# An attention and two-MoE kernel: merged float64 conversion, paired reciprocals, router dots over eight steps, an earlier gather

## The chip, the cores and the metric

The kernel runs on one core of a Trainium2 chip. A core has five engines with instruction queues of their own, which here are called PE (TensorE, the matrix unit), DVE (VectorE), ACT (ScalarE), POOL (GpSimd) and SP (SyncE, which here only issues DMA transfers). An engine works its queue in order and waits on semaphores for the others. The metric is the device time of one execution in microseconds, lower is better.

## The reference

```python
scores = scale * np.matmul(q, k.transpose(0, 1, 3, 2))      # q, k, v: 4 x 8 heads x 576 x 64
scores = np.where(mask, scores + bias[None], -1000000000.0) # causal window of 128, ALiBi slopes
attn = np.exp(scores - np.max(scores, axis=-1, keepdims=True))
attn = attn / (np.sum(attn, axis=-1, keepdims=True) + 1e-09)
x = np.matmul(attn, v)                                      # -> 2304 tokens x 512
a = x @ w_a; b = x @ w_b                                    # 512 -> 1536, weights in float64
x = (a * b @ w_out).astype(np.float32)                      # 1536 -> 512
logits = x @ w_gate + modality_bias[modality_id]            # 8 experts
e_idx = np.argmax(logits, axis=1)                           # one expert per token
gate_w = softmax(logits)[np.arange(N), e_idx]
out[mask] = gate_w[mask, None] * (np.maximum(x[mask] @ w1[e], 0.0) @ w2[e])   # for each expert e
```

## The kernel before

The 2304 tokens are 18 tiles of 128, taken in 7 chunks of 3, 2, 2, 3, 3, 3 and 2 tiles. Attention of a chunk is cut into items (a pair of heads and a tile). An item passes through: score_mm (PE), score_sel and score_max (DVE: mask and row maximum), score_exp (ACT: exponential p and its row sum), score_inv (DVE: 1e-9 added to the sum, then the reciprocal, both on the tile mx), the transpose ps_p (PE), its copy pc (ACT, DVE), a masked select pt (POOL), the product ps_o with v (PE), its scaled copy u (DVE and ACT), and for chunk 0 a transpose ps_ot back into xr, the input of the first MoE.

Each chunk then takes 12 steps j, one for each 128 columns of d_ff. A step has 24 matmuls mm_ab (a and b against xr, into ps_ab), asb (ACT copies a), gf (DVE multiplies it with b), g (ACT and DVE split gf in two parts), and mm_out of the step before into the accumulators. The attention of the next chunk runs between these matmuls. Chunk 0's attention has nothing to run beside, and is called the front. After it, slot0 runs chunk 0's steps.

The weights come as float64. On the chip they are read as pairs of 32-bit words and made into float32 bit by bit on DVE: `one` shifts and masks the high word (L429), `two` and `three` merge the sign and the low word into it (L433, L437). ACT then copies the result rounded (L444) and DVE subtracts that from it (L445), so that a weight is the sum of two parts. f64_ops does it for a tile of 128x512; wab_jobs makes a list of these jobs for a and b of a step, the two loads of which (wraw) SP issues one after the other (L450). In the front conv_step takes jobs off the list, in chunk 0 slot0 takes those of the step j+2 (NCV is 2). The bit tiles f64f stand in the tag "x2" with three buffers.

The router's logits of a chunk are computed during the steps of the next chunk. rd_fetch loads two experts' gate weights, sent to all partitions (wgt, 512 KB, on SP's queue, in the tag "wo" with four buffers, which it shares with the w_out tiles). rd_dot multiplies and sums them with every token tile on DVE (L596), rd_fin picks the expert. That takes the steps j = 0 to 3. Chunk 3 also writes zero rows through SP (x2_init).

At the end the second MoE runs in units of up to 384 tokens that share an expert: gen0 prepares the first, big(u) the next. A unit loads an index list (SP), gathers its tokens with an indirect DMA (POOL), and transposes them (ps_t) for the matmuls ps_h and ps_y.

The order within the engines' queues is written out by hand in the front, and found by a tile scheduler everywhere else, which places instructions by an estimate of when they are ready. So a small edit can move instructions far from it.

## Time and the profile before

| | |
|---|---|
| three runs | 837.05, 837.06, 839.56 us; median 837.06 |
| the profiled execution's own time | 840.08 us |
| its span, first to last instruction | 838.4 us (1.7 us lie around it) |
| mean granted PE clock | 0.994 |
| busy in the span | PE 812.3 us (97%), DVE 557.2 (66%), ACT 429.8 (51%), POOL 182.1 (22%) |

Busy is the time in which an engine has an instruction under way; a PE that is busy need not be at its peak, since matmuls are pipelined and their ends are modelled. Where an engine other than PE idles it costs nothing by itself. The profiled execution is one run, longer than the median of the three.

### The profile page before, as it was taken

The page shows a single profiled execution, that of the slowest core. Times are in us where ns is not written, and L with a number is a line of the kernel's source. Part 1 is how long each engine was busy: PE and PEld are TensorE (multiplying, and loading weights), DVE is VectorE, ACT ScalarE, POOL GpSimd, SP SyncE. Part 2 cuts the span into 40 slices and gives each one's busy share as a digit, 9 for nine tenths or more (in the row PEclk, how much of TensorE's full clock was granted, in tenths as well). Part 3 has the DMA queues.
Part 4 walks back from the last instruction along what each step waited for, and adds up shares of the span by engine and source line. Part 5 has one row for each costly group of instructions (what it writes and reads, how often), then busy time and mean ns, then how long its engine had stood idle before and what let it go on. Part 6 is the DMA issues. An engine that isn't in the chain of part 4 may idle for free.

```text
span 838.4 us, 14297 instructions
## 1 busy us (share of the span) xinstructions
PE 812.3 (97%) x4770; PEld 730.6 (87%) x4770; DVE 557.2 (66%) x1699; ACT 429.8 (51%) x1144; POOL 182.1 (22%) x245
## 2 busy tenths in 40 slices
PE   8899999999999989999999999999999999999994
PEld 6788877989989979999999999999988998979893
DVE  7799996987976875568865693377376444447320
ACT  6754465647666735665556632232336444537420
POOL 5322012113222222212222111100133030115101
PEclk9999999999999999999999999999999999999998
DMA  9995445786674774444642253647328553538301
GB/s 260 339 401 188 137 140 169 206 284 200 190 213 149 186 211 131 117 120 139 180 130 89 76 186 105 200 163 223 134 82 303 193 185 123 185 117 294 123 27 40
DMA packets 67874, 145.37 MB, mean 173 GB/s; under 512 B 12047, under 2 KB 32175, under 8 KB 67792
## 3 DMA queue, kind: packets, MB, share of 16 engines
q1 hardware_dynamic: 64240, 134.64, 51.6%
q0 software_dynamic: 3552, 9.73, 3.2%
q8 instruction: 40, 0.66, 0.3%
q14 instruction: 42, 0.34, 0.1%
HBM read 122.35 MB, written 22.12 MB: 172 GB/s over the span
## 4 chain that ended last, share of the span: by engine, by line
PE 75%; issue 8%; DMA 5%; DVE 5%; ACT 3%; POOL 2%; SPq 1%; POOLq 0%; ACTq 0%; DVEq 0%
PE ps_ab L512 32%; PE acc L529 13%; PE ps_h L1129 8%; PE ps_y L1112 7%; PE ps_o L369 4%; PE acc L525 4%; PE ps_s L247 2%; DMA wgt<-in_wgt 2%; PE ps_p L297 1%; PE ps_o L334 1%; PE ps_t L934 1%; PE ps_s L243 1%; DVE junk L596 1%; ACT p L271 1%; POOL out L1119 1%
## 5 line engine op out<-in xcount | busy, mean ns | idle before, releaser
L512 PE MATMUL ps_ab<-xr,wab 128*128 128x384 f32 (+1 forms) x2016 | 345.1, 318 | 4.7 <-DVE gf L1071 3.2
L512 PEld LDWEIGHTS ps_ab<-xr,wab 128*128 128x128 f32 x2016 | 308.5, 188 | 16.9 <-DVE gf L1071 4.7
L529 PE MATMUL acc<-wo,g 128*128 128x512 f32 x540 | 143.9, 398 | 0.0
L311 POOL TENSOR_SCALAR_AFFINE_SELECT pt<-pc 128x512 fp32r<-128x512 f32 (+1 forms) x72 | 50.4, 700 | 330.1 <-DVE pc L309 189.6
L529 PEld LDWEIGHTS acc<-wo,g 128*128 128x128 f32 x540 | 96.5, 188 | 15.3
L1129 PE MATMUL ps_h<-xT,w1s 128*128 128x384 f32 x576 | 104.2, 337 | 0.0
L1112 PE MATMUL ps_y<-w2s,h 128*128 128x512 f32 x432 | 104.1, 394 | 0.0
L1129 PEld LDWEIGHTS ps_h<-xT,w1s 128*128 128x128 f32 x576 | 99.7, 188 | 1.4 <-issue 0.5
L596 DVE CUSTOM_DVE_ANT_0 junk<-x,wgt 128x512 f32<-128x512 f32 x128 | 91.8, 717 | 12.2 <-DMA wgt<-in_wgt 8.0
L1112 PEld LDWEIGHTS ps_y<-w2s,h 128*128 128x128 f32 x432 | 79.8, 188 | 15.8
L271 ACT ACTIVATE p<-p,mx 128x128 f32<-128x128 f32 x144 | 56.8, 396 | 31.3 <-DVE mx L261 30.7
L1074 ACT CAST g<-gf 128x256 fp32r<-128x256 f32 (+1 forms) x72 | 33.0, 458 | 58.2 <-DVE gf L1071 57.9
L1071 DVE TENSOR_TENSOR gf<-ps_ab,asb 128x256 f32<-128x256 f32 (+1 forms) x72 | 35.1, 487 | 38.1 <-PE ps_ab L512 34.3
L1067 ACT COPY asb<-ps_ab 128x256 f32<-128x256 f32 (+1 forms) x72 | 30.6, 424 | 58.2 <-PE ps_ab L512 57.4
L885 DVE TENSOR_TENSOR w2s<-wr,w2s 128x1024 fp32r<-128x1024 f32 x24 | 29.4, 1225 | 38.4 <-ACT w2s L884 38.1
L313 POOL TENSOR_SCALAR_AFFINE_SELECT pt<-pc 128x512 fp32r<-128x512 f32 (+1 forms) x72 | 54.7, 760 | 0.0
L885 DVE TENSOR_TENSOR w1s<-wr,w1s 128x1024 fp32r<-128x1024 f32 x28 | 34.3, 1224 | 23.9 <-ACT w1s L884 23.9
L284 ACT ACTIVATE p<-p,mx 128x128 f32<-128x128 f32 x104 | 36.0, 394 | 25.3 <-DVE mx L276 23.8
L369 PE MATMUL ps_o<-pt,vv 128*128 128x256 f32 x312 | 48.8, 290 | 0.0
...
L255 DVE COPY_PREDICATED ps_s<-upper,ps_s 128x256 f32<-128x256 uint8 x72 | 30.5, 424 | 23.8 <-PE ps_s L247 16.5
L1132 ACT ACTIVATE h<-ps_h 128x384 fp32r<-128x384 f32 x48 | 23.4, 489 | 43.7 <-PE ps_h L1129 43.7
...
## 6 DMA issues: line engine op xcount, KB each, us to landing
wo<-wo_d SPq DMA_DIRECT2D x60, 512.0 KB, 3.8
wr<-in_moe_w SPq DMA_DIRECT2D x56, 512.0 KB, 4.3
wgt<-in_wgt SPq DMA_DIRECT2D x24, 512.0 KB, 4.3
wraw<-in_moe_w_a SPq DMA_DIRECT2D x12, 512.0 KB, 8.4
wraw<-in_moe_w_b SPq DMA_DIRECT2D x12, 512.0 KB, 9.1
wor<-in_moe_w_out SPq DMA_DIRECT2D x12, 512.0 KB, 4.4
...
wo_d<-wo SPq DMA_DIRECT2D x12, 512.0 KB, 3.3
```

What stands on the lines that cost most here:

```text
L271: nc.scalar.activation(out=it.p[:, h, :], in_=it.p[:, h, :], func=AF.Exp, bias=it.mx[:, 2 + h:3 + h], scale=-1.0, accum_out=it.mx[:, 4 + h ...
L284: nc.scalar.activation(out=it.p[:, h, :], in_=it.p[:, h, :], func=AF.Copy, scale=it.mx[:, 6 + h:7 + h])
L311: nc.gpsimd.affine_select(out=it.pt[:, :, 0], in_=pc, pattern=pat + [[-1, P]], base=0, channel_multiplier=1, compare_op=ALU.is_gt, fill=0.0)
L313: nc.gpsimd.affine_select(out=it.pt[:, :, 1], in_=pc, pattern=pat + [[1, P]], base=0, channel_multiplier=-1, compare_op=ALU.is_ge, fill=0.0)
L369: nc.tensor.matmul(it.po, lhsT=a.vv[:, t + b, r].rearrange("p h d -> p (h d)"), rhs=it.pt[:, :, b, s, :], start=(i == 0), stop=(i == 5))
L512: nc.tensor.matmul(ps[:, :n], lhsT=w[:, m, r, kk * P:(kk + 1) * P], rhs=xr[:, s, kk, :n], start=(idx == 0), stop=(idx == len(terms) - 1))
L529: nc.tensor.matmul(acc[c, t], lhsT=g[:, r, t * P:(t + 1) * P], rhs=w[:, s, :], start=(j == 0 and idx == 0), stop=(j == NJ - 1 and idx == 2))
L596: nc.vector.tensor_tensor_reduce(out=junk, in0=x2[:, 0:DM], in1=wgt[:, k], scale=1.0, scalar=0.0, op0=ALU.mult, op1=ALU.add, accum_out=lgr ...
L885: nc.vector.tensor_tensor(out=dst[:, 1], in0=srcw, in1=dst[:, 0], op=ALU.subtract)
L1071: nc.vector.tensor_tensor(out=gf[:, :n], in0=psb[:, :n], in1=asb[:, :n], op=ALU.mult)
L1112: nc.tensor.matmul(pss[t], lhsT=h[:, r, f, t * P:(t + 1) * P], rhs=W2[f // 2][:, s_, f % 2, :], start=(f == 0 and i == 0), stop=(f == 7 an ...
L1129: nc.tensor.matmul(ps, lhsT=W1[f // 2][:, r, kk, (f % 2) * P:(f % 2 + 1) * P], rhs=xT[:, s_, kk, :], start=(kk == 0 and i == 0), stop=(kk ...
```

## The change

Five edits. (1) wab_jobs converts a and b of a step together: one bit tile f64f of 128x1024 (tag "ff", one buffer), four jobs instead of eight, ACT's rounded copy in one instruction. conv_step takes one job each time and leaves four. (2) In the chunks 0 and 1 (V32) two items share a tile mx, and score_inv works once for both, at the second. (3) rd_dot does one expert a step over the steps j = 0 to 7; a fetched wgt is held for two steps; rd_fin comes at j = 7. (4) big(u) issues the index load and the gather of the unit behind it at a place S_P = 10 inside its own work, and not at that unit's start. (5) The memory for the descriptors of indirect DMAs is 8192 bytes, half of before, which makes room in SBUF for the larger f64f.

```diff
     def score_sel(it):
-        it.mx = at.tile([P, 8], F32, tag="mx", bufs=4, name="mx")
+        if a.c in V32 and cur_mx:
+            it.mxp, it.half = cur_mx.pop(), 1
+        else:
+            it.mxp, it.half = at.tile([P, 2, 8], F32, tag="mx", bufs=3, name="mx"), 0
+            if a.c in V32:
+                cur_mx.append(it.mxp)
+        it.mx = it.mxp[:, it.half]
...
     def score_inv(it):
+        if it.a.c in V32:
+            if it.half:
+                m = it.mxp
+                nc.vector.tensor_scalar(out=m[:, :, 4:6], in0=m[:, :, 4:6], scalar1=1e-9, scalar2=None, op0=ALU.add)
+                nc.vector.reciprocal(out=m[:, :, 6:8], in_=m[:, :, 4:6])
+            return
...
     def wab_jobs(j):
-        fs = []
-        def sp(m):
-            if m == 0:
-                wab[j] = wab_p.tile([P, 2, 2, KD * P], F32R, tag=f"wab{j}", name=f"wab{j}")
-            f64_split(fs[m], wab[j][:, m], nc.vector)
-        r = wraw[j]
-        return (f64_ops(r[:, 0].rearrange("p k f t -> p (k f) t"), 0, fs) +
-                f64_ops(r[:, 1].rearrange("p k f t -> p (k f) t"), 1, fs) + [("s", lambda: sp(0)), ("s", lambda: sp(1))])
+        r = wraw[j].rearrange("p m k f t -> p (m k f) t")
+        st = []
+        def one():
+            f = m1.tile([P, 2, KD * P], U32, tag="ff", bufs=1, name="f64f")
+            st.append(f)
+            nc.vector.tensor_scalar(out=f.rearrange("p m n -> p (m n)"), in0=r[:, :, 1], scalar1=3,
+                                    scalar2=0x3FFFFFFF, op0=ALU.logical_shift_left, op1=ALU.bitwise_and)
+        def more(k, sc, op):
+            f = st[0].rearrange("p m n -> p (m n)")
+            nc.vector.scalar_tensor_tensor(out=f, in0=r[:, :, k], scalar=sc, in1=f, op0=op, op1=ALU.bitwise_or)
+        def sp():
+            f = st[0].bitcast(F32)
+            w = wab[j] = wab_p.tile([P, 2, 2, KD * P], F32R, tag=f"wab{j}", name=f"wab{j}")
+            nc.scalar.copy(out=w[:, :, 0], in_=f)
+            nc.vector.tensor_tensor(out=w[:, :, 1], in0=f, in1=w[:, :, 0], op=ALU.subtract)
+        return [("d", one), ("d", lambda: more(1, 0xC0000000, ALU.bitwise_and)),
+                ("d", lambda: more(0, 29, ALU.logical_shift_right)), ("s", sp)]
...
     def rd_dot(wgt, e):
-        for k in range(2):
-            for i, t, x2, lgr in rd:
+        for i, t, x2, lgr in rd:
...
         def conv_step(g):
-            if g >= CVS and len(conv) > 8:
+            if g >= CVS and len(conv) > 4:
+                conv.pop(0)[1]()
...
-            if rd and R0 <= j < R0 + E // 2:
-                wgt = rd_fetch(2 * (j - R0))
+            if rd and R0 <= j < R0 + E and (j - R0) % 2 == 0:
+                wgt = rd_fetch(j - R0)
...
+    def pre_gather(u):
+        pool = side()
+        pre[u] = (pool,) + u_gather(ld(uv, NBIG + u, E * RG - UT), 3, pool)
...
+            if ahead and n_ == S_P:
+                pre_gather(u + 1)
...
-    nc = bacc.Bacc("TRN2", target_bir_lowering=False, num_devices=1)
+    nc = bacc.Bacc("TRN2", target_bir_lowering=False, num_devices=1, dynamic_dma_scratch_size=8192)
```

Where the order moves, it is shown at three places, row by row as the instructions stand in a queue. "waits" names the semaphores (DMAHW are queue places of transfers that SP issued).

DVE in the front, where the first conversion begins; mx is the tile of an item's maxima and sums, wraw_168 are the loads of step 0, u is the scaled copy of the first product with v. Before:

```order
L261 ISA p,mx<-ps_s,m_first 128x128
L261 ISA mx 128x1
L275 TENSOR_SCALAR mx<-mx 128x2 [waits Activation_49]
L276 RECIPROCAL mx<-mx 128x2 [waits DVE_49]
L429 TENSOR_SCALAR f64f<-wraw_168 128x512 [waits DMAHW1_49]
L341 TENSOR_SCALAR u<-ps_o,mx 128x64 [waits PE_49]
```

After:

```order
L269 ISA p,mx<-ps_s,m_first 128x128
L269 ISA mx 128x1
L287 TENSOR_SCALAR mx<-mx 128x2x2 [waits Activation_49]
L288 RECIPROCAL mx<-mx 128x2x2 [waits DVE_49]
L472 TENSOR_SCALAR f64f<-wraw_168 128x1024 [waits DMAHW2_49,DMAHW1_49]
L356 TENSOR_SCALAR u<-ps_o,mx 128x64 [waits DVE_49,PE_49]
```

The add and the reciprocal stand only at the second item of a pair and do both. The conversion is twice as wide and waits for two loads instead of one; u stands behind it as before.

DVE at the start of chunk 0; wraw_197 and wraw_208 are the loads of the steps 1 and 2, ps_s is the score of an item of chunk 1, and the ISA rows with p are its maxima. Before:

```order
L429 TENSOR_SCALAR f64f<-wraw_197 128x512 [waits DMAHW5_49]
L429 TENSOR_SCALAR f64f<-wraw_197 128x512 [waits DMAHW6_49]
L429 TENSOR_SCALAR f64f<-wraw_208 128x512 [waits DMAHW7_49]
L255 COPY_PREDICATED ps_s<-upper,ps_s 128x2x128 [waits DVE_49,PE_49]
L433 SCALAR_TENSOR_TENSOR f64f<-wraw_197,f64f 128x512 [waits DVE_49] x2
L433 SCALAR_TENSOR_TENSOR f64f<-wraw_208,f64f 128x512 [waits DVE_49]
L261 ISA p,mx<-ps_s,m_strad 128x128 [waits DVE_49]
L261 ISA mx 128x1
```

After:

```order
L472 TENSOR_SCALAR f64f<-wraw_197 128x1024 [waits DMAHW6_49,DMAHW5_49]
L263 COPY_PREDICATED ps_s<-upper,ps_s 128x2x128 [waits DVE_49,PE_49]
L477 SCALAR_TENSOR_TENSOR f64f<-wraw_197,f64f 128x1024 [waits DVE_49]
L269 ISA p,mx<-ps_s,m_strad 128x128 [waits DVE_49]
L269 ISA mx 128x1
L269 ISA p,mx<-ps_s,m_strad 128x128
L269 ISA mx 128x1
L477 SCALAR_TENSOR_TENSOR f64f<-wraw_197,f64f 128x1024 [waits DVE_49]
```

Ahead of the first maximum there were six conversion instructions of 512 columns, and now two of 1024.

SP in chunk 5, at the router's fetches; wo are the w_out tiles. Before:

```order
L588 DMA wgt<-in_wgt 128x1024 [waits PE_49]
L178 DMA vr_3_5934<-in_v 128x3x128 [waits DMAHW5_49,DMAHW2_49,DVE_49]
L492 DMA wo<-wo_d 128x1024 [waits DMAHW6_49,PE_49]
L588 DMA wgt<-in_wgt 128x1024 [waits DMAHW7_49,DMAHW1_49,PE_49]
L492 DMA wo<-wo_d 128x1024 [waits DMAHW4_49,DMAHW0_49,DVE_49]
L588 DMA wgt<-in_wgt 128x1024 [waits DMAHW3_49,PE_49]
L492 DMA wo<-wo_d 128x1024 [waits DMAHW7_49,DVE_49]
L588 DMA wgt<-in_wgt 128x1024 [waits DMAHW6_49,PE_49]
```

After:

```order
L611 DMA wgt<-in_wgt 128x1024 [waits DMAHW4_49,PE_49]
L178 DMA vr_3_5832<-in_v 128x3x128 [waits DMAHW5_49,DMAHW0_49,DVE_49]
L515 DMA wo<-wo_d 128x1024 [waits DMAHW7_49,DMAHW6_49,PE_49]
L515 DMA wo<-wo_d 128x1024 [waits DMAHW1_49,PE_49]
L611 DMA wgt<-in_wgt 128x1024 [waits DMAHW4_49,DVE_49]
L515 DMA wo<-wo_d 128x1024 [waits DMAHW3_49,PE_49]
L515 DMA wo<-wo_d 128x1024 [waits DMAHW6_49,DMAHW2_49,PE_49]
L611 DMA wgt<-in_wgt 128x1024 [waits DMAHW0_49,DVE_49]
```

The fetches of wgt waited for PE before; two of the three now wait for DVE. On DVE stands at the third of them, with x the token tiles and lgr their logits:

```order
L618 ISA junk,lgr<-x_6066,wgt 128x512 [waits DVE_49]
L618 ISA lgr 128x1
L324 TENSOR_TENSOR pc<-ps_p,pc 128x2x128 [waits Activation_49]
L618 ISA junk,lgr<-x_6060,wgt 128x512 [waits DMAHW3_49,DVE_49]
L618 ISA lgr 128x1
L1090 TENSOR_TENSOR gf<-ps_ab_6363,asb 128x384 [waits PE_49]
L618 ISA junk,lgr<-x_6063,wgt 128x512 [waits DVE_49]
```

The dot that waits for a DMA is the first on the new wgt, and gf of the next step is queued behind it.

## Rows read from the trace of the kernel before

**Rows 1.** Windows: stretch, length, busy (instructions) by engine, PE clock, DMA share, GB/s.

```profile
0.00:40.00 40.00, 34.95 (x188) 26.23 (x188) 32.28 (x156) 28.15 (x100) 19.59 (x60) 0.96 0.96 295
40.00:50.00 10.00, 8.95 (x51) 7.65 (x50) 7.83 (x23) 3.85 (x14) 2.24 (x4) 1.00 1.01 408
50.00:150.00 100.00, 100.00 (x522) 81.58 (x522) 92.92 (x239) 55.56 (x158) 17.31 (x24) 1.00 0.58 189
...
150.00:350.00 200.00, 194.42 (x1320) 180.74 (x1318) 156.14 (x547) 125.75 (x390) 48.59 (x62) 1.00 0.66 192
...
sum 838.00, PE 812.30 PEld 730.63 DVE 557.25 ACT 429.77 POOL 182.10; mean PE 101.54 PEld 91.33 DVE 69.66 ACT 53.72 POOL 22.76
```

**Rows 2.** Waits of PE over the span: us in total, times, longest.

```profile
PE ps_ab L512 <- DVE gf L1071: 3.2, 3, 2.0
PE ps_t L934 <- DMA xg<-x2d,idx: 1.6, 1, 1.6
PE ps_p L297 <- ACT p L271: 1.3, 6, 0.4
...
PE ps_o L334 <- POOL pt L311: 0.7, 2, 0.5
```

**Rows 3.** Groups of DVE by shape: busy us, mean ns, idle before.

```profile
L596 DVE CUSTOM_DVE_ANT_0 junk<-x,wgt 128x512 f32<-128x512 f32 x128 | 91.8, 717 | 12.2 <-DMA wgt<-in_wgt 8.0 <-ACT x L610 2.5
L885 DVE TENSOR_TENSOR w1s<-wr,w1s 128x1024 fp32r<-128x1024 f32 x28 | 34.3, 1224 | 23.9 <-ACT w1s L884 23.9
...
L433 DVE SCALAR_TENSOR_TENSOR f64f<-wraw,f64f 128x512 uint32<-128x512 uint32 x24 | 16.1, 690 | 0.0
L445 DVE TENSOR_TENSOR wab<-f64f,wab 128x512 fp32r<-128x512 f32 x24 | 15.9, 691 | 0.6 <-ACT wab L444 0.6
L275 DVE TENSOR_SCALAR mx<-mx 128x2 f32<-128x2 f32 x72 | 15.7, 219 | 7.6 <-ACT p L271 7.5
...
L276 DVE RECIPROCAL mx<-mx 128x2 f32<-128x2 f32 x72 | 11.4, 159 | 0.9
L429 DVE TENSOR_SCALAR f64f<-wraw 128x512 uint32<-128x512 uint32 x24 | 10.6, 469 | 0.6 <-DMA wraw<-in_moe_w_a 0.6
```

**Rows 4.** Timeline of SP, 11 to 13 us: start, us, instruction.

```profile
11.38 0.38 SPq L706 DMA_DIRECT2D wg<-in_moe_w_gate  x1
12.69 0.34 SPq L707 DMA_DIRECT2D mb<-in_moe_modality_bias  x1
```

**Rows 5.** Timeline of DVE at the first conversion; in brackets idle before.

```profile
11.38 0.52 DVE L429 TENSOR_SCALAR f64f<-wraw 128x512 uint32<-128x512 uint32 x1 [0.63 <-DMA wraw<-in_moe_w_a]
```

**Rows 6.** Timeline of POOL, 17 to 19 us.

```profile
17.37 0.84 POOL L311 TENSOR_SCALAR_AFFINE_SELECT pt<-pc 128x256 f32<-128x256 f32 x1 [3.77 <-ACT pc L303]
18.17 0.41 POOL L313 TENSOR_SCALAR_AFFINE_SELECT pt<-pc 128x256 f32<-128x256 f32 x1
```

**Rows 7.** Windows: the stretch of the front with the lower clock.

```profile
18.64:22.05 3.41, 3.41 (x14) 2.94 (x13) 1.89 (x9) 1.62 (x8) 2.67 (x8) 0.50 0.99 380
```

**Rows 8.** Timeline of DVE at the start of chunk 0.

```profile
43.25 1.28 DVE L429 TENSOR_SCALAR f64f<-wraw 128x512 uint32<-128x512 uint32 x3
...
46.58 0.28 DVE L261 CUSTOM_DVE_ANT_0 p<-ps_s,m_strad 128x128 f32<-128x128 f32 x1
```

**Rows 9.** Timelines of SP, DVE and PE in chunk 3, 293 to 305 us.

```profile
293.55 0.54 SPq L588 DMA_DIRECT2D wgt<-in_wgt  x1
...
301.70 0.69 DVE L596 CUSTOM_DVE_ANT_0 junk<-x,wgt 128x512 f32<-128x512 f32 x1 [5.96 <-DMA wgt<-in_wgt]
...
302.92 2.00 PE L512 MATMUL ps_ab<-xr,wab 128*128 128x384 f32 x10 [1.97 <-DVE gf L1071]
```

**Rows 10.** DMA issues of the page: KB each, median us from issue to landing.

```profile
wgt<-in_wgt SPq DMA_DIRECT2D x24, 512.0 KB, 4.3
```

**Rows 11.** Timeline of DVE in chunk 6: two steps' gf.

```profile
593.16 0.42 DVE L1071 TENSOR_TENSOR gf<-ps_ab,asb 128x256 f32<-128x256 f32 x1 [0.87 <-issue]
...
597.38 0.42 DVE L1071 TENSOR_TENSOR gf<-ps_ab,asb 128x256 f32<-128x256 f32 x1 [2.90 <-PE ps_ab L512]
```

More of the change, by code (lines that the diff above doesn't have):

```diff
@@ L232, in attn_moe_moe2 @@
         pass
+    cur_mx = []
     def score_mm(a, t):
@@ L426, in one @@
         def one():
-            f = m1.tile([P, 4 * P], U32, name="f64f", **(dict(tag="wo", bufs=WOB) if key == "o" else dict(tag="x2", bufs=X2B)))
+            f = m1.tile([P, 4 * P], U32, tag="wo", bufs=WOB, name="f64f")
             st.append(f)
@@ L441, in f64_ops @@
         return [("d", one), ("d", two), ("d", three)]
-    def f64_split(f, w, lo_eng):
-        nc.scalar.copy(out=w[:, 0], in_=f)
-        lo_eng.tensor_tensor(out=w[:, 1], in0=f, in1=w[:, 0], op=ALU.subtract)
     def wab_load(j):
@@ L592, in rd_dot @@
     def rd_dot(wgt, e):
-        for k in range(2):
-            for i, t, x2, lgr in rd:
-                junk = m1.tile([P, DM], F32, tag="x2T", bufs=1, name="junk")
-                nc.vector.tensor_tensor_reduce(out=junk, in0=x2[:, 0:DM], in1=wgt[:, k], scale=1.0, scalar=0.0,
-                                               op0=ALU.mult, op1=ALU.add, accum_out=lgr[:, e + k:e + k + 1])
+        for i, t, x2, lgr in rd:
+            junk = m1.tile([P, DM], F32, tag="x2T", bufs=1, name="junk")
+            nc.vector.tensor_tensor_reduce(out=junk, in0=x2[:, 0:DM], in1=wgt[:, e % 2], scale=1.0, scalar=0.0,
+                                           op0=ALU.mult, op1=ALU.add, accum_out=lgr[:, e:e + 1])
     def rd_fin():
@@ L794, in conv_step @@
         def conv_step(g):
-            if g >= CVS and len(conv) > 8:
-                kd = conv[0][0]
-                for _ in range(2 if kd == "s" else 1):
-                    if conv and conv[0][0] == kd:
-                        conv.pop(0)[1]()
+            if g >= CVS and len(conv) > 4:
+                conv.pop(0)[1]()
         ns = n0 + 2
@@ L987, in V @@
                     a_pv(live.pop(g))
-        dq(jw[:4], "d")
+        dq(jw[:2], "d")
         psa = mm_ab(c, j, 0, None if j else 1)
@@ L998, in slot0 @@
                 score_exp(sg)
-        dq(jw[4:], "d")
+        dq(jw[2:], "d")
         if act:
@@ L1086, in attn_moe_moe2 @@
             a_preps(g + 1)
-            if rd and R0 <= j < R0 + E // 2:
-                rd_dot(wgt, 2 * (j - R0))
-                if j == R0 + E // 2 - 1:
+            if rd and R0 <= j < R0 + E:
+                rd_dot(wgt, j - R0)
+                if j == R0 + E - 1:
                     rd_fin()
@@ L1284, in u_small, with big @@
             in_=y[0:HT], in_offset=None, bounds_check=N - 1, oob_is_err=False))
-    S_A, S_B, S_C = 20, 27, 4
-    def big(u, after=None, cont=None):
+    S_A, S_B, S_C, S_P = 20, 27, 4, 10
+    pre = {}
+    def pre_gather(u):
+        pool = side()
+        pre[u] = (pool,) + u_gather(ld(uv, NBIG + u, E * RG - UT), 3, pool)
+    def big(u, after=None, cont=None, ahead=False):
         ev = ld(uv, u, E - 1)
-        pool = side()
-        idx, xg = u_gather(ld(uv, NBIG + u, E * RG - UT), 3, pool)
+        if u not in pre:
+            pre_gather(u)
+        pool, idx, xg = pre.pop(u)
         W1, W2 = u_w1(ev, wrq), u_w2(ev, wrq)
@@ L1313, in attn_moe_moe2 @@
     for u in range(NFIX):
-        gs = big(u, 0 if u == SAT - 1 else None, gs)
+        gs = big(u, 0 if u == SAT - 1 else None, gs, u + 1 < NFIX)
     def ldx(col):
```

## The prediction

> **What bounds the kernel now.** I read the busy time of the engines in stretches first [rows 1]. TensorE (PE) is busy for 812.30 of 838.00 us; between 50 and 150 us it is never idle. A gain can therefore come only from the places where it is idle: 5.05 us in 0-40, 1.05 us in 40-50, 5.58 us in 150-350. Second the waits of PE [rows 2], which say who ends that idle time: VectorE's product gf (3.2 us in three waits), ScalarE's p, and once the gather xg of the first unit. VectorE is busy for 557.25 us of the span, but for 32.28 of the first 40 us and for 92.92 of the 100 us of 50-150: only there, and where its work comes in bursts, can it hold PE back. Third the rows of VectorE by shape [rows 3], which price what is removed. Last the places where PE waited: the front [rows 4 to 7], the start of chunk 0 [rows 8] and chunk 3 [rows 9].
>
> **Conversion of two tiles at once.** Of 24 x 4 instructions of 512 columns, 12 x 4 of 1024 remain. The trace has no merged conversion, so its price is bounded: twice the row of 512 from above (no gain), and from below by how VectorE's subtraction grows from 512 to 1024 columns, 691 to 1224 ns [rows 3]: a fixed part of .16 us goes with each merged pair. By that the bit operations cost about .78 us (from .469) and 1.22 us (from .690), and a tile saves 4 x .16 = .63 us (0 to .63). I take .63, because the row of 1224 ns is the same kind of instruction. One tile is converted in the front, eleven in chunk 0. The Trainium skill's "VectorE: DVE Perf Modes", section "The TRN2 errata — SBUF-src ops pay a fixed extra latency per instruction", says that instructions on SBUF data pay a fixed cost apiece, measured there at about 150 cycles; the subtraction's .16 us agrees in size, so a sum by the page would be the same.
>
> What the merge costs is a wait. Before, the first bit operation needs only a's half: it starts at 11.38 us when that lands, after .63 us of idling [rows 5]. After, it waits for b's half too. SyncE's next two loads reuse the same two queue places and are issued at 11.38 and 12.69 [rows 4], so b's half lands 1.31 us after a's. Behind the waiting instruction stands u of the first pv item, which PE's transposes and ScalarE wait for; with the longer operation u comes about 1.31 + .31 = 1.6 us later.
>
> **Reciprocals in pairs.** 20 items of chunks 0 and 1 had an add (219 ns) and a reciprocal (159 ns) each [rows 3]; ten pairs go, 10 x .378 = 3.8 us of VectorE, six of them (2.3 us) in the front.
>
> **Sum for the front (0-40).** VectorE loses 1.6 us at 11.4 us and gains .63 + 2.3 = 2.9 us until 40. The loss comes first, the gain later, and PE's own items follow u. I take -0.5 us. Best case: all 2.9 us come out of PE's 5.05 us idle, -2.9. Worst: the 1.6 us stay. There is a second cost with bounds: PE's granted clock is .50, the lower of its two levels, from 18.64 to 22.05 [rows 7], after short stalls; those 3.41 us hold 1.7 us of full-speed work, so the front gets 1.7 us dearer if a later u brings one more such stretch. Ends -2.9 and +3.3.
>
> **Port.** POOL's two selects of a masked tile read SBUF. The same select takes .84 us at 17.37, while a two-input VectorE operation is under way, and .41 us at 18.17 [rows 6]. With merged operations of 1.22 us instead of .69 a select can be held .53 us longer, four times in the front: 0 to +2.1 us. I take 0, because PE waited for POOL's tiles only .7 us in two waits [rows 2]. The Trainium skill's "SBUF — State Buffer", section "Who interferes with whom", says why: the pair of ports that VectorE and GpSimd share is held for a whole instruction and the loser is blocked. By that rule alone the front would come out 2.1 us later; it is weighed below as part of a rival.
>
> **Start of chunk 0.** Before, three bit operations (1.28 us together), a select and three bit operations of the second kind stand ahead of the first max: 43.25 to 46.58 is 3.33 us [rows 8], and p behind that max makes PE wait [rows 2]. After, one bit operation of .78, the select and one of 1.22 stand there: about 2.3 us. So max comes 1.0 us earlier, and I take PE's whole 1.05 us of 40-50 [rows 1]: -1.0 (-1.05 to 0). **Rest of chunk 0:** VectorE saves 11 x .63 us and four pairs, but PE is never idle there [rows 1], so 0. The cover could go: the shared f64f has one buffer instead of three, and tile 3 is ready only just before its step. Ends -2 (waits hidden in PE's modelled busy time) and +1.
>
> **Router dots over eight steps.** A dot is .717 us [rows 3] and a short read; four or six stand in one step before, two or three after, over twice as many steps. The number is the same, so VectorE's work is too, but half the burst. PE's stalls in 150-350 lie in these bursts. Chunk 3's is the largest: the third weight fetch is issued at 293.55, behind a k load that waits for a buffer, and lands 8.15 us later; VectorE idles 5.96 us, and PE 1.97 us on gf [rows 9]. After, the second fetch still stands behind that load, but the load is free earlier, since kk comes sooner in the step, and the dots behind the fetch are half as many. I take the 1.97 us, -2.0 (-2.8 with a wait that follows from it; to 0). For the rest of the idle time in 150-350, 5.58 - 2.8 = 2.8 us, about half: -1.3 (-2.8 to 0).
>
> **What the spreading adds.** The order shows a new wait: ten of the 24 fetches now stand behind VectorE's own dots. They reuse the buffer of the fetch before them, which is held for two steps, so the fetch is issued only when its last dot is done, and the next dot is 2 to 16 instructions behind. A fetch takes 4.3 us [rows 10], plus some .4 us of issuing. So VectorE will idle for wgt in about eight places, 1 to 4 us each, 12 to 20 us in all (before, the row of the dots has 8.0 us [rows 3]). Queued behind the waiting dot are the next gf, g and max. In three-tile chunks PE's order leaves some 4 us and more before it needs that gf, and the idle time fits. In chunk 6 a step is only 4.22 us [rows 11]. There the last dot is done some 1.25 us after gf starts (.42 and .8), the fetch lands at 1.25 + 4.7 = 5.95, dot and next gf are done at 7.2, and PE needs that gf a step and two thirds after the first, at 7.0. So +0.2 there and as much in the other place of chunk 6: +0.5 in all. Lower end 0, upper end +8, if they land in 8.15 us as in chunk 3.
>
> **Units' gather.** SyncE's and POOL's order in the units is the same before and after: the index load still stands behind the weights in front of it. Only the first unit's gather moves, ahead of three scatters. The change does nothing here: 0 (ends -1.6, the whole wait for xg [rows 2], and +1.6, as much again if the halved descriptor memory slows a gather).
>
> **Sum.** -0.5 - 1.0 + 0 - 2.0 - 1.3 + 0.5 + 0 = -4.3 us against the profiled execution's own 840.08 us, so 835.8. That execution is 3.02 us above the median of the runs, 837.06. What it has more may be chunk 3's late landing itself, which costs 2.8 us: then the -2.0 is not to be had in the median run, and 837.06 - 2.3 = 834.8; else 837.06 - 4.3 = 832.8. I choose **833.5 us**.
>
> **Rivals.** (A) No change: PE is the bound, its idle time moves with the order, 834.5 to 839.6. For it: 97% busy, and gains of VectorE in chunk 0 that buy nothing. With the terms of chunks 1 to 5 at 0 and +0.5 for the new waits, 837.06 - 1.0 = 836. (B) Slower, by the new waits for weights: if the fetches land as late as at 301.70, VectorE's dots block gf past PE's need. 3.85 us more at each of the two places in chunk 6, and 1.5 to 2 in chunks 1 and 5, is +8: 833.5 + 8 = 841.5. It decides from a landing of about 5 us on; against it speaks the median of 4.3. (C) Slower in the front: u 1.6 us late, one more stretch at the lower clock, the selects held 2.1 us: +3.3 + 2.1 instead of -0.5, 839.4. The first ab matmul would come 3 us later or more. For it: the chain p, pt, u has no slack in the front; against it: VectorE makes 2.9 us good by its end. (D) More gain: 150-350 loses all its 5.6 us of idle time and the front 2.9, 837.06 - 5.6 - 2.9 + .5 = 829. For it: VectorE has less to do wherever it is late; against it: some of that idle time is ScalarE's.
>
> **How the numbers follow.** Within 0.3% (2.5 us) of 837.06 a measurement can't tell a change. My forecast (831 to 834.5) .43, D .12, A .28, B .12, C .05. So faster (under 834.5) .55, within 0.3% .29, slower .16: half of C falls within. The range takes in A whole and the front of B: 829.0 to 840.0.
>
> **What would show it.** Right: first bit operation of 1024 columns at 12.7 us and about .78 us long, the others 1.2 us; max of the first score in chunk 0 about 1 us earlier after it; PE idle under .3 us in 40-50; VectorE's idle for wgt rising from 8.0 to 12-20 us in eight or more waits, PE's wait for gf below 1.5 us. Wrong: PE waiting more than 3 us for gf with wgt landing over 5 us (B); the first ab matmul over 1 us later than before (C); merged operations of 1.38 us, twice the old, so that nothing is saved.

## The result: slower by 0.9%, and the profile after

The changed kernel took 846.74 us (median of 6 runs, 843.45 to 847.86) against 837.3 us (6 runs, 834.63 to 839.77) of the kernel before on the same chip: ratio 1.0091, 95% interval 1.0063 to 1.0118. (A ratio here is the estimate on record over all runs; the quotient of the two medians is 1.0113.) Its profiled execution took 845.16 us with a span of 843.5, 5.1 us more than the profiled execution before. The medians differ by 9.4 us, so the rows below hold little more than half of the loss; where the rest lies no kept trace shows.

The windows of the changed kernel show where PE lost it (columns as in [rows 1]):

```profile
0.00:40.00 40.00, 35.23 (x187) 26.67 (x187) 30.46 (x140) 27.70 (x98) 20.71 (x60) 0.96 0.96 291
40.00:50.00 10.00, 10.00 (x57) 8.80 (x58) 7.50 (x23) 5.24 (x21) 2.80 (x6) 1.00 1.02 409
50.00:150.00 100.00, 99.50 (x521) 81.23 (x520) 92.40 (x187) 52.82 (x142) 18.16 (x24) 1.00 0.57 193
150.00:250.00 100.00, 94.52 (x686) 86.93 (x685) 82.65 (x281) 62.66 (x195) 25.27 (x29) 1.00 0.68 205
250.00:350.00 100.00, 97.23 (x615) 90.54 (x614) 67.85 (x255) 62.68 (x196) 23.05 (x31) 1.00 0.65 176
350.00:580.00 230.00, 227.43 (x1347) 211.60 (x1346) 145.76 (x490) 107.54 (x307) 42.86 (x53) 1.00 0.44 134
```

PE's idle time is a window's length less its first number. The same windows of the kernel before give 97.25, 97.17 and 230.00 busy us for the last three. So the idle time went from 5.05 to 4.77, 1.05 to 0, 0 to .50, 2.75 to 5.48, 2.83 to 2.77, and 0 to 2.57: a gain of 1.3 us up to 50 us, as forecast, and losses of 2.7 us in 150 to 250, which holds most of chunk 1 and the first half of chunk 2, and of 2.6 us in 350 to 580, where chunk 4 starts. Chunk 3 gave nothing.

The waits of PE and the one of VectorE that matters, in the changed kernel ([rows 2] and the first row of [rows 3] before):

```profile
PE ps_ab L535 <- DVE gf L1090: 5.6, 8, 1.7
PE ps_o L384 <- POOL pt L326: 2.8, 2, 2.3
PE ps_t L953 <- DMA xg<-x2d,idx: 1.3, 2, 1.0
...
DVE junk L618 <- DMA wgt<-in_wgt: 33.5, 14, 6.9
```

VectorE waits for router weights four times as long as before, 14 times instead of 3, and PE waits for gf 5.6 us instead of 3.2. There are three places to look at. Steps 6 and 7 of chunk 1, the timelines of SP (two rows), DVE (five rows) and PE (last row), with the idle time and its releaser in brackets:

```profile
171.96 0.38 SPq L178 DMA_DIRECT2D vr<-in_v  x1
172.43 0.46 SPq L611 DMA_DIRECT2D wgt<-in_wgt  x1
...
177.97 0.69 DVE L618 CUSTOM_DVE_ANT_0 junk<-x,wgt 128x512 f32<-128x512 f32 x1 [1.68 <-DMA wgt<-in_wgt]
...
184.80 1.21 DVE L192 TENSOR_TENSOR kk<-kr,kk 128x1024 fp32r<-128x1024 f32 x1
...
187.11 0.70 DVE L618 CUSTOM_DVE_ANT_0 junk<-x,wgt 128x512 f32<-128x512 f32 x1
187.84 0.62 DVE L215 SCALAR_TENSOR_TENSOR qq<-qr,qscale,qq 64x384 fp32r<-64x384 f32 x1
...
188.64 0.42 DVE L1090 TENSOR_TENSOR gf<-ps_ab,asb 128x256 f32<-128x256 f32 x1
...
189.12 1.10 PE L535 MATMUL ps_ab<-xr,wab 128*128 128x256 f32 x7 [1.70 <-DVE gf L1090]
```

The fetch leaves at 172.43, right behind a v load (vr) that had held SP's queue for 3.7 us while it waited for VectorE, and lands 5.5 us later. VectorE loses 1.68 us at 177.97 and has no gap from there to gf: the late dots run into kk and qq, the preparation of the next keys and queries, and gf comes when PE has been idle for 1.7 us. The stall stands 11 us behind the wait that caused it.

Chunk 3, timelines of DVE, SP, DVE and PE, which answer to [rows 9]:

```profile
294.10 1.13 DVE L618 CUSTOM_DVE_ANT_0 junk<-x,wgt 128x512 f32<-128x512 f32 x1
...
295.27 0.34 SPq L611 DMA_DIRECT2D wgt<-in_wgt  x1
...
303.79 0.69 DVE L618 CUSTOM_DVE_ANT_0 junk<-x,wgt 128x512 f32<-128x512 f32 x1 [6.94 <-DMA wgt<-in_wgt]
...
305.01 1.31 PE L535 MATMUL ps_ab<-xr,wab 128*128 128x384 f32 x6 [1.07 <-DVE gf L1090]
```

The fetch is issued at 295.27, when the last dot on the weights before it is done (294.10 + 1.13): the new wait has taken the place of the k load's. And the landing is 8.5 us after the issue, as it was 8.1 us before, where the median is 4.0: the DMA engines are busy throughout (the DMA share is 1.11 in the window 290 to 295 us and 1.07 in 295 to 300), with six writes of zero rows (x2_init) and two k loads issued from 286 us on. No run took those writes away, so that they are the reason is not shown.

The start of chunk 4, timelines of DVE, POOL and PE:

```profile
382.87 1.23 DVE L192 TENSOR_TENSOR kk<-kr,kk 128x1024 fp32r<-128x1024 f32 x1
384.13 1.26 DVE L215 SCALAR_TENSOR_TENSOR qq<-qr,qscale,qq 64x384 fp32r<-64x384 f32 x2
385.42 0.42 DVE L324 TENSOR_TENSOR pc<-ps_p,pc 128x256 fp32r<-128x256 f32 x1
...
385.92 1.03 POOL L326 TENSOR_SCALAR_AFFINE_SELECT pt<-pc 128x512 fp32r<-128x512 f32 x1 [12.46 <-DVE pc L324]
...
387.00 0.63 PE L384 MATMUL ps_o<-pt,vv 128*128 128x256 f32 x3 [2.35 <-POOL pt L326]
```

Here no weight is late. kk and qq stand ahead of pc in VectorE's order, 2.5 us of work, and PE waits 2.35 us for the select behind pc. In the kernel before kk stands at 376.35, well ahead. This stall is the scheduler's order; runs 9 and 10 below, which can have no late weight, have it too.

### The profile page after: what moved, and what is told of

It is laid out like the page before. It is cut to its first block, busy times and chain, and to the rows that moved or that the text cites. A ratio compares the mean times of both kernels' runs of the same rounds, so it can differ in the third digit from the quotient of the medians.

```text
span 843.5 us, 14190 instructions
## 1 busy us (share of the span) xinstructions
PE 813.3 (96%) x4770; PEld 730.4 (87%) x4770; DVE 551.3 (65%) x1631; ACT 427.4 (51%) x1132; POOL 184.5 (22%) x245
## 4 chain that ended last, share of the span: by engine, by line
PE 69%; DVE 9%; issue 9%; DMA 7%; ACT 4%; POOL 2%; SPq 1%; POOLq 0%; DVEq 0%; ACTq 0%
PE ps_ab L535 29%; PE acc L552 11%; PE ps_y L1131 7%; PE ps_h L1148 7%; PE acc L548 4%; PE ps_o L384 4%; PE ps_s L249 2%; DMA wgt<-in_wgt 2%; DVE junk L618 2%; DMA wr<-in_moe_w 2%; PE ps_p L312 1%; PE ps_o L349 1%; DMA idx<-tab 1%; PE ps_s L245 1%; DVE qq L215 1%
## 5 line engine op out<-in xcount | busy, mean ns | idle before, releaser
L326 POOL TENSOR_SCALAR_AFFINE_SELECT pt<-pc 128x512 fp32r<-128x512 f32 (+1 forms) x72 | 52.7, 732 | 341.9 <-DVE pc L324 225.9
L618 DVE CUSTOM_DVE_ANT_0 junk<-x,wgt 128x512 f32<-128x512 f32 x128 | 91.0, 711 | 41.1 <-DMA wgt<-in_wgt 33.5
L328 POOL TENSOR_SCALAR_AFFINE_SELECT pt<-pc 128x512 fp32r<-128x512 f32 (+1 forms) x72 | 56.2, 780 | 0.0
L384 PEld LDWEIGHTS ps_o<-pt,vv 128*128 128x128 f32 x312 | 42.5, 189 | 6.1 <-POOL pt L326 3.6
L1094 DVE TENSOR_TENSOR g<-gf,g 128x256 fp32r<-128x256 f32 (+1 forms) x72 | 39.1, 542 | 12.0 <-ACT g L1093 11.7
```

The source lines that it names most:

```text
L326: nc.gpsimd.affine_select(out=it.pt[:, :, 0], in_=pc, pattern=pat + [[-1, P]], base=0, channel_multiplier=1, compare_op=ALU.is_gt, fill=0.0)
L328: nc.gpsimd.affine_select(out=it.pt[:, :, 1], in_=pc, pattern=pat + [[1, P]], base=0, channel_multiplier=-1, compare_op=ALU.is_ge, fill=0.0)
L384: nc.tensor.matmul(it.po, lhsT=a.vv[:, t + b, r].rearrange("p h d -> p (h d)"), rhs=it.pt[:, :, b, s, :], start=(i == 0), stop=(i == 5))
L618: nc.vector.tensor_tensor_reduce(out=junk, in0=x2[:, 0:DM], in1=wgt[:, e % 2], scale=1.0, scalar=0.0, op0=ALU.mult, op1=ALU.add, accum_out ...
L1094: nc.vector.tensor_tensor(out=gt[:, 1, :n], in0=gf[:, :n], in1=gt[:, 0, :n], op=ALU.subtract)
```

## The experiments

All runs stand against runs of the kernel before on the same chip (medians 838 to 840 us). "From before" means the kernel before with one edit. The table has the time (median), the ratio to before with its interval, VectorE's idle time for wgt and PE's for gf (us, in how many waits), and how many stretches of PE at the lower granted clock (.50) lie between 150 and 800 us; the last three columns are read from each run's profiled execution. The kernel before has 8.0 in 3, 3.2 in 3 and none, the changed kernel 33.5 in 14, 5.6 in 8 and none.

| run | us | ratio | idle for wgt | PE for gf | clock |
|---|---|---|---|---|---|
| 1 after, dots over 4 steps | 838.75 | 0.9995 [0.9977, 1.0012] | 9.9 in 4 | 5.4 in 4 | 1 |
| 2 before, dots over 8 | 849.58 | 1.0120 [1.0091, 1.0148] | 34.3 in 15 | 4.0 in 3 | 3 |
| 3 before, merged conversion | 840.54 | 1.0004 [0.9987, 1.0021] | 6.3 in 2 | 1.1 in 2 | 1 |
| 4 dots 8, tag wo of 5 | 848.36 | 1.0097 [1.0068, 1.0125] | 25.3 in 9 | 5.5 in 3 | 3 |
| 5 dots 8, one expert a fetch | 863.55 | 1.0277 [1.0245, 1.0310] | 60.9 in 31 | 6.9 in 8 | 1 |
| 6 dots 8 in chunks 3 to 6 | 850.05 | 1.0122 [1.0092, 1.0153] | 30.0 in 12 | 1.3 in 2 | 2 |
| 7 dots 8 in chunks 1 and 2 | 848.55 | 1.0107 [1.0072, 1.0142] | 15.4 in 6 | 4.4 in 4 | 3 |
| 8 run 1, first tile in halves | 839.10 | 0.9993 [0.9973, 1.0013] | 6.6 in 2 | 1.0 in 2 | 0 |
| 9 dots 4, no fetch | 871.75 | 1.0395 [1.0365, 1.0426] | 0 | 3.2 in 3 | 1 |
| 10 dots 8, no fetch | 871.58 | 1.0398 [1.0374, 1.0422] | 0 | 3.2 in 4 | 0 |
| 11 dots 8, own 2 buffers | 848.73 | 1.0115 [1.0090, 1.0140] | 21.6 in 17 | 5.8 in 7 | 2 |
| 12 dots 4, tag wo of 5 | 845.73 | 1.0101 [1.0072, 1.0129] | 7.0 in 2 | 1.0 in 2 | 1 |
| 13 dots 4, own 1 buffer | 852.13 | 1.0158 [1.0132, 1.0183] | 38.6 in 18 | 8.1 in 6 | 2 |
| 14 dots 8, own 1 buffer | 856.27 | 1.0215 [1.0189, 1.0240] | 35.8 in 16 | 7.2 in 7 | 2 |

**Which edit (runs 1 to 3).** Run 1 is the changed kernel with rd_dot and its two calls as before, run 2 the kernel before with those of the change, run 3 the kernel before with the merged conversion and the smaller descriptor memory. The edit of run 1 at the fetch:

```diff
-            if rd and R0 <= j < R0 + E and (j - R0) % 2 == 0:
-                wgt = rd_fetch(j - R0)
+            if rd and R0 <= j < R0 + E // 2:
+                wgt = rd_fetch(2 * (j - R0))
```

> The changed kernel with the router's dots put back (two experts a step over the steps j = 0 to 3, a fetch each step); merged conversion, paired reciprocals, gather and descriptor memory stay changed. Theory D (the dots over eight steps lose the time: fetches that wait for VectorE's own dots, and dots that now share steps 4 to 7 with kk, qq and rd_fin): the loss goes and the gain of the chunk 0 start stays, about 836 us, 10 below the changed kernel; VectorE's idle time for wgt falls from 33.5 us to under 10. Rival S (any edit reshuffles the scheduled order and costs some us somewhere): it stays above 841. Rival C (the merged conversion loses it): it stays at about 846.

> The kernel before with the dots over eight steps alone. Theory D: slower than before by 6 to 11 us, 843 to 848, with VectorE idle for wgt 25 us or more and TensorE waiting for gf 5 us or more, above all in chunks 1 and 3. Rival S: within 3 us of before, either way. Rival C: as before, 837.

> The kernel before with the merged conversion alone (and the smaller descriptor memory that makes room for it). Theory D: faster by 0 to 2 us, 835 to 837: the wait for b's half costs some 2 us at 20 us and is made good by 50. Rival S: 838 to 842. Rival C: about 846.

The spread is the edit that loses the time: without it the changed kernel is level with before (0.9995), and alone it costs all of it (1.0120). The four other edits together are worth 0 within about .2%. Run 2 also shows why a stall of 1.7 us can cost twice that. Timeline of its PE at the place of chunk 1, then windows that begin at or in three of its stalls (1.76, 1.27 and 2.34 us):

```profile
189.56 1.82 PE L512 MATMUL ps_ab<-xr,wab 128*128 128x256 f32 x12 [1.76 <-DVE gf L1070]
...
190.48:195.00 4.52, 4.52 (x24) 4.14 (x23) 4.52 (x32) 2.67 (x10) 1.62 (x2) 0.62 0.75 246
244.00:250.00 6.00, 5.35 (x29) 4.96 (x29) 2.63 (x11) 2.46 (x9) 0.75 (x1) 0.72 0.63 185
391.00:397.00 6.00, 5.12 (x22) 5.12 (x23) 5.86 (x15) 4.28 (x15) 3.74 (x4) 0.72 0.47 127
```

The mean granted clock is .62 over 4.52 us and .72 over 6 us: each time some 1.7 us of full-speed work is lost besides the stall (.38 x 4.52 and .28 x 6). In the changed kernel's profiled execution the same stall of 1.70 us at 189.12 was followed by no such stretch, so the loss is not fixed. Its six executions had mean granted clocks between .987 and .994, the profiled one .994: the other five were at the lower clock for longer than the rows show. That is not all of the difference between them, for the time does not follow the clock alone (843.45 us at .991, 847.25 at .993).

**Late fetches or the spread (runs 13, 14, 9, 10).** Runs 13 and 14 make every fetch wait for the last dot of the fetch before it, with four and with eight steps. Runs 9 and 10 take the fetches away: the weights of the experts 0 and 1 are loaded once and used for all eight, so that other tokens go to other experts and the second MoE is longer; these two are compared with one another. Runs 4 and 9 to 14 also have the smaller descriptor memory, for room.

```diff
-        wgt = m1.tile([P, 2, DM], F32, tag="wo", bufs=WOB, name="wgt")
+        wgt = m1.tile([P, 2, DM], F32, tag="wgt", bufs=1, name="wgt")      # runs 13, 14
...
+        if not wgt_one:                                                    # runs 9, 10
+            wgt = m1.tile([P, 2, DM], F32, tag="wgt", bufs=1, name="wgt")
             nc.sync.dma_start(out=wgt.rearrange("p e d -> p (e d)"),
                               in_=w_gate_t[e:e + 2].rearrange("(o e) d -> o (e d)", o=1).partition_broadcast(P))
+            wgt_one.append(wgt)
+        return wgt_one[0]
```

> The kernel before, dots over four steps, with the weights of two experts loaded once at the start into a tile of its own and used for all eight (the other experts' weights are left out, so the routing and the length of the second MoE differ; compare with the next run, which routes alike). No dot can wait for a fetch. It is the base for the next run; its stall at 302 us, where a late fetch held VectorE, should be gone.

> The same with the dots over eight steps; weights left out as in the run before, same routing. If the late fetches are the loss: as long as the run before within 2.5 us. If the place of the dots in the steps 4 to 7 is the loss (beside kk, qq and rd_fin, and by the order of the attention around them): 5 us or more longer, with TensorE falling back between 180 and 190 us again.

> The kernel before, its dots over four steps as they were, but the pair of weights wgt in a tag of its own with one buffer, so that every fetch waits for the last dot of the fetch before it (and the descriptor memory of 8192 bytes, which makes room). Theory L (the time goes to fetches that wait for DVE's own dots, whatever the number of steps): DVE's idle for wgt rises from 8 us to 30 us or more in over 10 waits, PE's waits for gf to over 6 us, and the kernel is 8 to 20 us slower than before, 845 to 857. Theory S (the spread over eight steps itself costs, by the order that it makes): DVE idles as much, but the time stays within 4 us of before. Theory O (any change of the order costs some 8 us): 843 to 848 with no place where PE waits for a gf behind a dot that waits for wgt.

> The same one buffer for wgt, with the dots over eight steps. Theory L: each step has half as many dots behind a late fetch, but four fetches per chunk wait as before; DVE idles 25 to 45 us for wgt, the time is 845 to 857 and within 5 us of the run with four steps. Theory S: over 845 here while the run with four steps stays under 841. Theory O: the two differ by chance, up to 8 us, not in the order of their idle times for wgt.

Without fetches eight steps cost what four do (871.58 and 871.75). PE waits some 14 us at one place of the second MoE in both, where a difference could be lost, so the end of the first MoE is the better mark. The first and last start (us) of PE's matmuls into ps_ab, behind their durations in ns, for the kernel before, run 2, run 9 and run 10:

```profile
L512 PE MATMUL ps_ab<-xr,wab x2016: 274/336/741, 40.8 to 601.3; 128*128 128x384 f32 x106, 128*128 128x256 f32 x78
L512 PE MATMUL ps_ab<-xr,wab x2016: 276/336/741, 39.9 to 613.3; 128*128 128x384 f32 x106, 128*128 128x256 f32 x78
L512 PE MATMUL ps_ab<-xr,wab x2016: 276/336/741, 40.8 to 604.4; 128*128 128x384 f32 x106, 128*128 128x256 f32 x78
L512 PE MATMUL ps_ab<-xr,wab x2016: 276/336/741, 40.5 to 603.8; 128*128 128x384 f32 x106, 128*128 128x256 f32 x78
```

With fetches the spread costs 12.0 us up to there (601.3 to 613.3), without them nothing (604.4 to 603.8), in one execution each; not all of the 12.0 us is late weights, for run 2 has the stall of chunk 4 and the kernel before has not. The stall at 302 us goes with the fetches, as expected: PE is busy for all of 250 to 350 in runs 9 and 10. At 189 us run 10 has .32 us of idle PE, where run 2 has 1.76. But run 9 is 3.1 us behind the kernel before, although no fetch in it can be late: the order has changed, and the stall of chunk 4 (2.35 us) is in it.

With late fetches four steps lose 13.3 us against before, with no spread at all. So theory L is right in its result: what costs is weights that land after VectorE is ready for them, and the spread matters because it makes more of them late. The reason that it gives for the lateness, a fetch that is issued only when VectorE's own dots free its buffer, is one of several. Of the 14 late fetches of the changed kernel eight wait for VectorE (19.6 of the 33.5 us) and six for PE, among them the one of chunk 1 above; run 2's at the same place waits for PE too. Run 13 shows the whole chain in chunk 2; waits of DVE and PE, then timelines of SP, DVE and PE, then the window behind the stall:

```profile
DVE junk L596 <- DMA wgt<-in_wgt: 38.6, 18, 6.7
...
PE ps_ab L512 <- DVE gf L1071: 8.1, 6, 3.2
...
233.93 0.68 DVE L596 CUSTOM_DVE_ANT_0 junk<-x,wgt 128x512 f32<-128x512 f32 x1
...
234.64 0.33 SPq L588 DMA_DIRECT2D wgt<-in_wgt  x1
...
238.94 0.69 DVE L596 CUSTOM_DVE_ANT_0 junk<-x,wgt 128x512 f32<-128x512 f32 x1 [1.98 <-DMA wgt<-in_wgt]
...
243.69 1.21 DVE L192 TENSOR_TENSOR kk<-kr,kk 128x1024 fp32r<-128x1024 f32 x1
...
246.56 0.42 DVE L1071 TENSOR_TENSOR gf<-ps_ab,asb 128x256 f32<-128x256 f32 x1
...
247.04 1.83 PE L512 MATMUL ps_ab<-xr,wab 128*128 128x256 f32 x12 [3.23 <-DVE gf L1071]
...
247.04:252.00 4.96, 4.96 (x25) 4.58 (x26) 3.48 (x29) 3.58 (x15) 1.51 (x2) 0.66 0.99 236
```

The last dot ends at 234.6, the fetch leaves at 234.64 and lands after 4.3 us, VectorE idles 1.98 us, its dots are pushed against kk and qq, gf comes at 246.56, PE idles 3.23 us and then runs at a mean clock of .66 for 4.96 us (1.7 us more). In run 14 it is 2.31 us at 191.14 in chunk 1, and chunk 4 has the stall of 2.32 us behind POOL as well, which run 13 has not. The two runs differ by 4.1 us; that is not all fetches.

**More buffers, or one fetch a step (runs 4, 5, 11, 12).** Run 4: WOB 5. Run 5: dots over eight steps, each with a fetch of one expert. Run 11: the same in a tag of its own with two buffers of half the size. Run 12: the kernel before with WOB 5.

```diff
-    WOB = 4
+    WOB = 5                                                                # runs 4, 12
...
-        wgt = m1.tile([P, 2, DM], F32, tag="wo", bufs=WOB, name="wgt")
+        wgt = m1.tile([P, 1, DM], F32, tag="wo", bufs=WOB, name="wgt")     # run 5
+        wgt = m1.tile([P, 1, DM], F32, tag="wgt", bufs=2, name="wgt")      # run 11
```

> The kernel before with the dots over eight steps, and five buffers instead of four in the tag that wgt shares with w_out's tiles (with the smaller descriptor memory for room). In the order, the fetches that wait for VectorE's dots fall from eleven to six, and lead by more instructions. If the late fetches are the loss (theory D, first half): 838 to 841, idle time for wgt under 15 us. If dots beside kk, qq and rd_fin in the steps 4 to 7 are the loss (theory D, second half): as slow as with four buffers, 843 or more.

> The kernel before with the dots over eight steps, but one expert's weights fetched a step (256 KB, a buffer of its own), so that no buffer is held for two steps and the next fetch need not wait for the last dot of the one before. If the fetches that wait for VectorE's dots are the loss: VectorE's idle time for wgt under 12 us and 838 to 841. If the place of the dots in the steps 4 to 7 is (they share them with kk, qq and rd_fin, and the scheduled order of the attention changes with them): 846 to 850 as with one fetch for two experts.

> Dots over eight steps with all weights, one expert a fetch, in a tag of its own with two buffers of 2 KB, so that a fetch leads by one whole expert's dots and w_out's tiles keep their four buffers. If late fetches are the loss: VectorE idle for wgt under 15 us and 838 to 842. If the place of the dots is: 845 or more in spite of it.

> The kernel before with dots over four steps and five buffers instead of four in the tag of wgt and w_out (smaller descriptor memory for room): the candidate for a better version. If fetch lead is what matters: idle time for wgt from 8 to under 3 us, no stall at 302 us, 834 to 837.5, faster than before by .3% or more. If before's stall there is hidden or moves elsewhere: within .2% of before.

None is a cure. A fifth buffer takes 9 us of the idle time away (34.3 to 25.3) and 1 us of the time, which is within the noise. Runs 4, 5 and 11 were to bring the idle time under 12 or 15 us, and left 25.3, 60.9 and 21.6, so they decide nothing between the theories. Run 5 doubled the number of fetches and of waits, and is the slowest: most of its late fetches leave 3 to 5 us ahead of their dot, and land too late (issued at 411.06, dot at 414.26 after 2.34 us of idling).

Run 12 missed both of its expectations: four steps, as little idle time for wgt as before (7.0 us in 2 waits), and 1.0101. Its PE lost time in chunk 3 behind ScalarE's p, and in chunk 4 by the stall seen above. Timelines of its DVE and PE in chunk 3, and a wait of its PE:

```profile
300.64 0.69 DVE L596 CUSTOM_DVE_ANT_0 junk<-x,wgt 128x512 f32<-128x512 f32 x1 [6.74 <-DMA wgt<-in_wgt]
...
302.57 0.33 PE L297 MATMUL ps_p<-ident,p 128*128 128x128 f32 x1 [3.71 <-ACT p L284]
...
PE ps_o L369 <- POOL pt L311: 2.3, 1, 2.3
```

The stall in chunk 3 has late weights behind it after all: behind the dot of 300.64 stands the reciprocal that ScalarE's p needs, and PE loses 3.71 us by a wait of 6.74, where before it lost 1.97 and .82 by one of 5.96. In chunk 4 kk stands at 382.25 ahead of pc at 384.80, as in the changed kernel; so it does in runs 9 and 10, which fetch nothing. So the order decides what a late fetch costs, and has a price of its own besides (2.35 us here).

**Where (runs 6 and 7).** The kernel before, with eight steps in the chunks 3 to 6 or in 1 and 2 alone:

```diff
+            ne = 1 if c in D8 else 2      # D8 = (3, 4, 5, 6) in run 6, (1, 2) in run 7
+            if rd and j < E // ne and j * ne % 2 == 0:
+                wgt = rd_fetch(j * ne)
```

> The kernel before with the dots over eight steps in the steps of chunks 3 to 6 alone; chunks 1 and 2 take four. In the run with the dots alone TensorE fell back 7.5 us in chunks 1 and 2 and some 4.5 us behind them, most of it at one place at the start of chunk 4. If these are separate losses: 841 to 845 here. If the order of the whole program decides, the place at chunk 4 need not come back: 837 to 840.

> The kernel before with the dots over eight steps in the steps of chunks 1 and 2 alone, where a step is 4.2 us and VectorE is over 80% busy. If losses are local and add up: 844 to 847, with TensorE falling back 4 us or more between 180 and 190 us. If the order of the whole program decides: anything from 838 on, and the fall between 180 and 190 need not come back.

Each half costs what the whole does (1.0122 and 1.0107 beside 1.0120; run 6 lies above both of its forecasts), so the losses don't add up: stalls are not a price for each late fetch. That they come where the order happens to have work of VectorE behind it fits the places seen, and is not tested by itself. Run 7 has the stall at 190 in chunk 1 again, run 6 has 5.88 us of idle PE in 250 to 350, behind a wait of 9.25 us for wgt.

**The front (run 8).** Run 1 with the first bit operation of step 0 in two halves, so that it needn't wait for b's load:

```diff
+        def half(m):
+            nc.vector.tensor_scalar(out=st[0][:, m], in0=wraw[j][:, m].rearrange("p k f t -> p (k f) t")[:, :, 1],
+                                    scalar1=3, scalar2=0x3FFFFFFF, op0=ALU.logical_shift_left, op1=ALU.bitwise_and)
+
+        first = [("d", lambda: half(0)), ("d", lambda: half(1))] if j == 0 else [("d", one)]
```

> The changed kernel with the router's dots as before, and the first bit operation of step 0 alone in two halves again, so that it does not wait for b's load. If the wait for b's half costs what it seems (TensorE 2.0 us late at 20 us): lateness at 20 us under .6 us, and of that 1 to 2 us last, 836.5 to 838, faster than before by some .3%. If the front makes it good anyway: as with the dots put back alone, within .15% of before.

The wait went and the time stayed (0.9993): the front's PE stalled later instead (1.38 us behind POOL, 1.00 us behind u) and then had the lower clock. Windows of its PE:

```profile
28.00:30.00 2.00, 1.73 (x9) 1.46 (x8) 1.38 (x9) 1.73 (x10) 0.88 (x3) 0.63 1.04 336
30.00:34.00 4.00, 4.00 (x17) 3.53 (x17) 2.21 (x10) 1.67 (x9) 1.27 (x4) 0.50 1.01 401
34.00:36.00 2.00, 2.00 (x11) 1.78 (x10) 1.90 (x4) 1.89 (x7) 1.83 (x5) 0.67 1.03 382
```

That is about 6.8 us at the lower clock, as in run 1 (6.83 us from 18.67), where the kernel before had 3.41 [rows 7].

## Why the prediction was wrong

The forecast was 833.5 us; the kernel took 846.74. Two steps failed, "Router dots over eight steps" with -2.0 and -1.3, and "What the spreading adds" with +0.5; a third loss, by the order in chunk 4, had no step at all.

**What the spreading adds.** The mechanism was named and its place was wrong. I expected 12 to 20 us of idle time for wgt in about eight places; it is 33.5 in 14. I priced it in chunk 6, where a step is short, and wrote that in three-tile chunks the idle time fits. Chunk 6 lost nearly nothing: VectorE idles up to 3.73 us there, and PE's only stall is .22 us. The price came in chunk 1, where gf stands behind dots, kk and qq, and behind a fetch that is not one of the ten that wait for VectorE. I had measured the slack to the next gf; what mattered was the work of VectorE in the following two steps. Rival B was right in its sign and, at 841.5, too small. It was to decide from a landing of 5 us on, and the median of 4.3 [rows 10], 4.0 after, was held against it; but the median hides the two fetches that PE paid for, which landed after 5.5 us (chunk 1) and 8.5 us (chunk 3). B's 1.5 to 2 us in chunk 1 is what came (1.70), its 7.7 in chunk 6 did not. At the other twelve places the landing took 3.4 to 5 us, and the fetch was issued too late for its dot. (Two sums of the prediction don't close: B's terms make 9.2 us or more, not 8, and with half of C "within 0.3%" is .305 and "slower" .145, not .29 and .16. The forecast doesn't rest on them.)

**Router dots.** Chunk 3 was to lose its late fetch. It kept 6.94 us of idle time (5.96 before), for two reasons: the fetch that VectorE waits for, now the second of the chunk, exchanged the k load for VectorE's own dot as the thing it waits for, and it took as long to land as before. I had thought that this late landing might belong to the one profiled execution; the longest wait for wgt is 4.7 to 9.2 us in every kept trace with fetches. PE's part of it fell from 1.97 to 1.07 us, which new stalls in the same window made up (2.83 and 2.77 us of idle PE in 250 to 350). The other -1.3, for the rest of 150 to 350, came out as about +2.7, the change of 150 to 250. In the order I had seen that ten fetches now wait for DVE, and did not apply that to the fetch on whose gain the largest term rested.

**What neither names.** Half of the loss that the rows show, 2.6 us in 350 to 580 with the stall of 2.35 us in chunk 4, has no step: the order shifts kk and qq ahead of pc. I read the order at three places and not there. And of a stall I priced only its own length outside the front, though [rows 7] showed a lower clock behind short stalls; in 12 of the 14 runs of the table one to three such stretches lie between 150 and 800 us.

**The start.** The merged conversion saves what was forecast. Groups of DVE by shape, changed kernel:

```profile
L477 DVE SCALAR_TENSOR_TENSOR f64f<-wraw,f64f 128x1024 uint32<-128x1024 uint32 x24 | 30.4, 1267 | 0.2
L483 DVE TENSOR_TENSOR wab<-f64f,wab 128x1024 fp32r<-128x1024 f32 x12 | 14.8, 1229 | 1.9 <-ACT wab L482 1.9
...
L472 DVE TENSOR_SCALAR f64f<-wraw 128x1024 uint32<-128x1024 uint32 x12 | 8.3, 696 | 1.6 <-DMA wraw<-in_moe_w_b 1.5
L287 DVE TENSOR_SCALAR mx<-mx 128x4 f32<-128x4 f32 x10 | 1.8, 180 | 0.0
L288 DVE RECIPROCAL mx<-mx 128x4 f32<-128x4 f32 x10 | 1.8, 176 | 0.2
```

By the rows of 512 columns a tile took 5.08 us, and takes .696 + 2 x 1.267 + 1.229 = 4.46 us: .62 saved, .63 predicted. A pair of the add and the reciprocal is .36 us for two items. The front's wait is there too, and the selects. Timelines of DVE and POOL:

```profile
12.84 0.69 DVE L472 TENSOR_SCALAR f64f<-wraw 128x1024 uint32<-128x1024 uint32 x1 [1.54 <-DMA wraw<-in_moe_w_b]
...
18.81 1.37 POOL L326 TENSOR_SCALAR_AFFINE_SELECT pt<-pc 128x256 f32<-128x256 f32 x1 [3.63 <-ACT pc L318]
...
22.98 1.40 POOL L328 TENSOR_SCALAR_AFFINE_SELECT pt<-pc 128x256 f32<-128x256 f32 x1
```

Front -.28 (forecast -.5) and start of chunk 0 -1.05 (forecast -1.0) were right; the first max stands 2.07 us behind the first bit operation, where it was 3.33 [rows 8]. Timeline of DVE, changed kernel:

```profile
43.53 0.68 DVE L472 TENSOR_SCALAR f64f<-wraw 128x1024 uint32<-128x1024 uint32 x1
...
45.60 0.28 DVE L269 CUSTOM_DVE_ANT_0 p<-ps_s,m_strad 128x128 f32<-128x128 f32 x1
```

But this is not kept. The idle time fell, yet the first matmul into ps_ab starts at 41.1 us, where it was 40.8, and runs 1 and 3, which have the merged conversion without the spread, end level with before: run 1 has 4.34 us of idle PE in 150 to 250, where before has 2.75. I had put the rest of chunk 0 at 0 and not asked what VectorE's earlier work moves later. The gather was right: nothing (PE's wait for xg 1.3 instead of 1.6 us).

**What stays open.** Why the same stall brings a stretch at the lower clock in one execution and not in another, and what makes the scheduler set kk and qq ahead of pc in chunk 4 in some kernels. Run 12 lost 1% without a new late fetch, so of the changed kernel's .9% the part of the late weights and that of the order can't be parted exactly: the rows give 2.7 us (150 to 250) and 2.6 us (350 to 580), and the 4 us by which the medians differ more than the profiled executions are in neither. A fetch issued well ahead, in place of the last wait, was not tried.
